# Two narrow first jobs, a last unit in halves, and an earlier 2 MB load in a fused attention kernel

## The chip, the cores and the metric

One core of one Trainium2 chip. The metric is device time in microseconds (us), the median over several executions of the whole program. Every run lists the mean granted clock of TensorE (1.0 is full speed). In the profiles PE is TensorE (matmuls), PEld its weight loads, ACT is ScalarE, DVE VectorE, POOL GpSimd, and SP SyncE, which issues most loads and stores. Ratios are the mean time of one kernel's fast runs over the mean of the other's in the same rounds on the same chip, so they are not quite the ratio of the medians quoted beside them.

## The reference

Two attention blocks over 2048 tokens, 1024 features and 32 heads of 32, results joined:

```python
# A: full softmax attention
scores = einsum('bhqd,bhkd->bhqk', q, k) * Dh ** (-0.5)
o = einsum('bhqk,bhkd->bhqd', softmax(scores), v)
out_A = o.transpose(0, 2, 1, 3).reshape(B, S, D) @ wo
# B: four segments of 512, causal attention in each, plus a memory M, z of the earlier ones
a_mem = (phi(q) @ M) / (phi(q) @ z + 1e-6)
o = g * a_mem + (1 - g) * a_dot          # g = sigmoid(beta)
# ... M and z are then updated from phi(k) and v; out_B = o @ wo
```

## The kernel before

A scheduler written in Python decides, while the program is built, the order of every instruction on every engine. It plans a chain of 621 score batches: PE multiplies QA by KA into PSUM (the buffer that matmuls write), ACT takes the exponential into a PT slot, PE multiplies PT by V and by ones (the row sums). Between the batches it places projection jobs (K, Q, V), output jobs and the memory work of block B. WoB holds the 2 MB of output weights of block B. Numbers in `par` steer the scheduler.

```python
par = dict(..., wob=80, oks=(1, 3, 5), pd=4, od=4, slk=0.3, ...)

def first_x(self):                        # the first four token tiles
    ...
    yield self.warm(8)                    # 8 matmuls of 512 columns on zeros, result unused
    for t in range(4):
        # 8 transposes of tile t into PSUM; after t == 1: self.warm(4)
        # DVE copies the tile to xA
    ...
def job(self, due, mm, keys, out, ...):   # a projection: 8 groups of 4 matmuls, n columns
    for i in range(last + 1):
        yield do("PE", lambda e: mm(e, i, bank, 0, n, st, sp), ...)
    yield do(eng, out, ...)               # DVE copies the result out of PSUM

def finish(...):                          # last unit: whole 256 queries at once
    # transpose(256), reciprocal, transpose(256), multiply -> OTA

yield ("ev", ("pos", self.par["wob"]))    # at this step of the chain
yield do("SP", lambda e: e.dma_start(self.WoB[:, :, :], ...), kb=2048)   # 2 MB in one load
```

## Time and profile before

| | before |
|---|---|
| time, median of 3 | 1099.28 us (1098.48 to 1099.56) |
| span of the profiled run, clock | 1097.8 us, 1.0 |
| start, to the first exponential | 10.40 us |
| ACT's idle time between exponentials | 4.67 us in seven gaps |
| tail, after the last exponential | 7.3 us |

The prediction below shows ACT's timeline and the tail. Here is PE's timeline where the 2 MB load of WoB is in flight. Columns: start, length, engine, line, operation, tiles, count, and in brackets the idle time before it with what ended it.

```profile
157.55 0.28 PE L1214 MATMUL ps<-PT,ones 128*32 128x256 bf16 x3
158.84 0.27 PE L1214 MATMUL ps<-PT,ones 128*32 128x256 bf16 x1 [1.01 <-issue]
```

PE stops after three of four matmuls that belong together. Nothing that the profile shows is awaited ("issue"). The second is a stretch of DVE and POOL at about 385 us:

```profile
383.05 1.22 DVE L884 SCALAR_TENSOR_TENSOR PH<-KQB,PH 128x1024 bf16<-128x1024 bf16 x1
...
386.26 0.42 DVE L1109 TENSOR_TENSOR PT<-PT,mask 128x512 bf16<-128x512 bf16 x1
...
387.03 0.72 POOL L891 TENSOR_SCALAR Zb<-maskbd,Mf 128x128 bf16<-128x128 f32 x1
```

### The profile page before, as it was taken

Reading aid. Unit: us, or ns where it says so; the run is one execution under the profiler, and the core shown is the slowest. Engines: PE = TensorE matmul, PEld = TensorE weight load, DVE = VectorE, ACT = ScalarE, POOL = GpSimd, SP = SyncE. Lnnn points to the kernel's source line nnn. Section 1 sums busy time; section 2 is a strip of 40 time slices with the busy share of each in tenths; the row PEclk is TensorE's granted clock in tenths of the full one; section 3 lists DMA queues with packets and bytes.
Section 4 is the critical chain, followed back from the end, with each engine's and each line's share of the span. In section 5 each row is a group of like instructions: output and inputs, shape, how many; then the busy total and the mean of one; then the engine's idle time right before and its main releaser. Section 6 shows DMA issues by size and latency. Waiting matters only on the chain.

```text
span 1097.8 us, 54247 instructions
## 1 busy us (share of the span) xinstructions
PE 1038.0 (95%) x25233; PEld 538.1 (49%) x25233; DVE 748.0 (68%) x1569; ACT 1077.1 (98%) x1188; POOL 127.4 (12%) x231
## 2 busy tenths in 40 slices
PE   8999999998999999999999998999999999899998
PEld 4545444444454445544454554544455444544454
DVE  2366666565778778887878789887748769543334
ACT  6999999999999999999999999999999999999997
POOL 2011110101102011110101121111102111100000
PEclk9999999999999999999999999999999999999999
DMA  9622361243302232243212242331122221201011
GB/s 189 102 61 56 75 139 30 52 92 64 72 27 53 59 61 48 50 85 70 56 42 55 42 84 46 73 63 35 48 65 56 51 46 22 84 32 36 31 41 67
DMA packets 213767, 67.49 MB, mean 61 GB/s; under 512 B 202786, under 2 KB 210978, under 8 KB 213538
## 3 DMA queue, kind: packets, MB, share of 16 engines
q1 hardware_dynamic: 212066, 63.07, 27.0%
q8 instruction: 199, 3.26, 1.3%
q10 hardware_dynamic: 1472, 0.92, 0.3%
q14 instruction: 30, 0.25, 0.1%
HBM read 36.70 MB, written 8.39 MB: 41 GB/s over the span
## 4 chain that ended last, share of the span: by engine, by line
ACT 83%; PE 12%; DVE 3%; DMA 1%; issue 0%; DVEq 0%
ACT PT L1099 82%; PE ps L719 4%; PE ps L1214 3%; PE ps L1068 2%; PE ps L1303 2%; DMA VA<-VT 1%; ACT OTA L1099 1%; PE ps L598 0%; DMA VB<-VT 0%; DVE VT L724 0%; ACT OTB L1099 0%; DVE PH L1137 0%; PE ps L646 0%; PE ps L899 0%; DVE OD L1256 0%
## 5 line engine op out<-in xcount | busy, mean ns | idle before, releaser
L1099 ACT ACTIVATE PT<-ps 128x1024 bf16<-128x1024 f32 x1164 | 1056.1, 1171 | 4.7 <-PE ps L1068 4.0
L1214 PE MATMUL ps<-PT,ones 128*32 128x256 bf16 (+2 forms) x4784 | 283.0, 268 | 1.0 <-issue 1.0
L1214 PE MATMUL ps<-PT,VA 128*32 128x256 bf16 x4016 | 241.4, 274 | 3.7 <-ACT PT L1099 1.4
L1068 PE MATMUL ps<-QA,KA 32*128 32x256 bf16 x4096 | 209.6, 273 | 31.0 <-ACT PT L1099 25.8
L719 PE MATMUL ps<-xB,WB 128*32 128x512 bf16 x3072 | 203.3, 381 | 3.4 <-DVE outsb L1308 0.9
L719 PE MATMUL ps<-xA,WA 128*32 128x512 bf16 (+1 forms) x3232 | 203.0, 371 | 3.1 <-DVE KA L724 0.6
L1068 PEld LDWEIGHTS ps<-QA,KA 32*128 32x128 bf16 x4096 | 62.8, 92 | 204.5 <-ACT PT L1099 189.7
L1214 PEld LDWEIGHTS ps<-PT,ones 128*32 128x32 bf16 x4784 | 128.0, 97 | 32.7 <-issue 16.0
L1214 PEld LDWEIGHTS ps<-PT,VA 128*32 128x32 bf16 x4016 | 107.3, 96 | 40.6 <-issue 22.0
L719 PEld LDWEIGHTS ps<-xA,WA 128*32 128x32 bf16 x3232 | 74.7, 96 | 76.0 <-issue 25.9
L719 PEld LDWEIGHTS ps<-xB,WB 128*32 128x32 bf16 x3072 | 71.0, 96 | 75.1 <-issue 30.0
L1256 DVE COPY OD<-ps 128x512 f32<-128x512 f32 x127 | 86.6, 682 | 24.3 <-PE ps L1214 23.5
L1308 DVE CAST outsb<-ps 128x512 bf16<-128x512 f32 x56 | 38.7, 690 | 77.9 <-PE ps L1303 75.5
L1111 POOL TENSOR_TENSOR PT<-PT,mask 128x256 bf16<-128x256 bf16 x64 | 46.6, 729 | 356.1 <-ACT PT L1099 354.0
L724 DVE CAST VT<-ps 128x512 bf16<-128x512 f32 x64 | 44.1, 688 | 63.1 <-PE ps L719 53.1
L724 DVE CAST KQB<-ps 128x512 bf16<-128x512 f32 x64 | 44.1, 689 | 54.2 <-PE ps L719 53.4
L1303 PE MATMUL ps<-WoB,OTB 128*32 128x512 bf16 x1024 | 67.2, 381 | 1.3 <-DVE OD L1256 1.0
L855 POOL COPY VZ<-VB 64x256 bf16<-64x256 bf16 x64 | 30.5, 476 | 299.7 <-DMA VB<-VT 256.8
L1262 DVE STREAM_TRANSPOSE OD<-Rall 128x256 f32<-128x256 f32 x127 | 55.7, 440 | 2.9
L1259 DVE STREAM_TRANSPOSE Dt<-OD 128x256 f32<-128x256 f32 x127 | 55.2, 436 | 2.2
L1303 PE MATMUL ps<-xA,OTA 128*32 128x512 bf16 x832 | 53.2, 381 | 0.0
L1214 PE MATMUL ps<-PT,VB 128*32 128x192 bf16 (+2 forms) x768 | 44.5, 240 | 4.8 <-DVE OD L1256 2.6
(111 smaller groups left out, 885.2 us busy)
## 6 DMA issues: line engine op xcount, KB each, us to landing
WB<-in_B_wk_dram SPq DMA_DIRECT2D x32, 256.0 KB, 3.0
WB<-in_B_wq_dram SPq DMA_DIRECT2D x32, 256.0 KB, 2.9
WB<-in_B_wv_dram SPq DMA_DIRECT2D x32, 256.0 KB, 3.1
out_dram<-outsb SPq DMA_DIRECT2D x63, 128.0 KB, 1.8
WA<-in_A_wqkv_dram SPq DMA_DIRECT2D x23, 256.0 KB, 3.3
WoB<-in_B_wo_dram SPq DMA_DIRECT2D x1, 2048.0 KB, 10.7
xA<-in_A_wo_dram SPq DMA_DIRECT2D x1, 2048.0 KB, 9.2
OTA<-in_A_x_dram SPq DMA_DIRECT2D x2, 256.0 KB, 5.0
```

What stands on the lines that cost most here:

```text
L719: ins = e.matmul(self.ps[32 * c:32 * c + 32, bank, lo:hi], W[:, i, 32 * c:32 * c + 32], x(i)[:, lo:hi], start=st, stop=sp)
L724: return e.tensor_copy(dst, self.ps[:, bank, 0:n])
L855: yield do("POOL", lambda e, j=j: e.tensor_copy(self.VZ[H * j:H * j + H, j:4:2, :], V[0:H, j:4:2, 0:P]), r=[("VB", n % 2)], w=["VZ"], cost ...
L1068: ins = e.matmul(out, l, r, start=a, stop=z)
L1099: yield do("ACT", lambda e: e.activation(to, self.ps[:, pr[0]:pr[1] + 1, 0:n], ACTF.Exp, scale=sc), r=[("ps", bk) for bk in pr], w=keys, c ...
L1111: yield do("POOL", lambda e: e.tensor_tensor(d, d, m, ALU.mult), r=keys + ["mask"], w=keys, cost=0.4 + sz * 0.0014, prio=0)
L1214: ins = e.matmul(out, l, r, start=st, stop=sp)
L1256: yield do("DVE", lambda e: e.tensor_copy(OD[:, :], self.ps[:, OB, :]), r=[("ps", OB)], w=[("OD", x), ("Rb", x)], cost=dve(2 * QU), prio=0 ...
L1259: yield do("DVE", lambda e: e.transpose(Dt[:, :], Rb), r=[("Rb", x)], w=[("Dt", x)], cost=dve(QU), prio=self.par["fp"], hold=0.15)
L1262: yield do("DVE", lambda e: e.transpose(Rb.rearrange("p (a b) -> p a b", b=32), self.spread(Rc)), r=[("Rc", ui % 64)], w=[("Rb", x)], cost ...
L1303: ins = e.matmul(self.ps[32 * c:32 * c + 32, bank, lo:hi], lhs(j)[:, 32 * c:32 * c + 32], W(j)[:, lo:hi], start=st, stop=sp)
L1308: return f(self.outsb[ob][:, :], self.ps[:, bank, :])
```

## The change

Its intent: begin the chain sooner, by letting the first K and Q jobs run on 128 tokens as soon as these are there; end it sooner, by normalising and projecting the last unit in two halves; and new numbers for the scheduler, which ask for WoB 20 steps sooner.

```diff
-    par = dict(... wob=80, oks=(1, 3, 5), pd=4, od=4, slk=0.3, ...)
+    par = dict(... wob=60, oks=(1, 4, 6), pd=6, od=0, slk=0.2, xp=0, wm=1, ...)
 def first_x(self):
-                yield self.warm(4)
+                yield self.warm(self.par["wm"])
 def job(...):
-        for i in range(last + 1):
+        for r, (lo, hi, xk, ev) in enumerate(ranges or [(0, n, [], None)]):
+            if ev:
+                yield ("ev", ev)
+            for i in range(last + 1):
+                fn = lambda e, ...: mm(e, i, bank, lo, hi, st, sp)
 # streams of group 0
-            streams = [[K and Q jobs], [V jobs]]
+            streams = {"K": todo[:1], "Q": todo[1:2], "rest": ..., "V": ...}
+            if g == c == 0 and w != "V":
+                ranges = [(0, P, [("xA", 0, t0)], None), (P, 2 * P, [("xA", 0, t0 + 1)], ("xt", 0, t0 + 1))]
 def finish(...):                          # last unit
-            # transpose(256), reciprocal, transpose(256), multiply
+            for tt in range(2):           # the same four on 128 queries, then
+                Q.fire(("finh", tt))      # the output jobs of this half may end
 # ... cut: bookkeeping of the events, order of the last output jobs
```

More of the change, by code (lines that the diff above doesn't have):

```diff
@@ L405 @@
 class Kernel:
-    par = dict(b=(16, 12, 9), mem=0, memM=2, span=60, rate=0.6, ahead=28, sl=7, pv=14, ob=4, lead=6, b0=1, bpos=16, wob=80, mg=0.05, off=0, oks=(1, 3, 5), sh=4, pd=4, o0=4, od=4, run=4, po=(1, 1), fp=2, fil=0.65, fs=0.15, ta=2, td=40, pvw=3, pvs=3, slk=0.3, pat=0.0, kh=3, mk=(0, 1, 1), mp=0, pe=3, tk=(0.5, 1))
+    par = dict(b=(16, 12, 9), mem=0, memM=2, span=60, rate=0.6, ahead=28, sl=7, pv=14, ob=4, lead=6, b0=1, bpos=16, wob=60, mg=0.05, off=0, oks=(1, 4, 6), sh=4, pd=6, o0=4, od=0, run=4, po=(1, 1), fp=2, fil=0.65, fs=0.15, ta=2, td=40, pvw=3, pvs=3, slk=0.2, pat=0.0, kh=3, xp=0, wm=1, mk=(0, 1, 1), mp=0, pe=3, tk=(0.5, 1))
     def __init__(self, nc, A_x, A_wqkv, A_wo, B_x, B_wq, B_wk, B_wv, B_wo, B_beta, out):
@@ L637, in first_x, with back @@
         pairs = yield acq(self.pairs, 3)
+        def back():
+            for t in range(4):
+                yield ("ev", ("xt", 0, t))
+                if t % 2:
+                    Q.give(self.pairs, [pairs[t // 2]])
+            Q.fire(("xA", 0))
+        Q.spawn(back())
         yield do("DVE", lambda e: e.memset(self.PT[:, 0, :], 0.0), w=[("PT", 0)], cost=0.3, prio=0)
@@ L647, in f @@
                 return ins
-            yield do("PE", f, r=[("XS", t), "ident"], w=[("ps", b)], cost=0.65, prio=0, mode=FULL)
+            yield do("PE", f, r=[("XS", t), "ident"], w=[("ps", b)], cost=0.6, prio=0 if t < 2 else self.par["xp"], mode=FULL)
             if t == 1:
-                yield self.warm(4)
+                yield self.warm(self.par["wm"])
                 Q.give(self.pairs, [pairs[2]])
@@ L654, in first_x @@
             Q.spawn(self.one(do("DVE", lambda e, s=src, d=dst: e.tensor_copy(d, s), r=[("ps", b)], w=[("xA", 0, t)], cost=0.6, prio=0), t))
-        for t in range(4):
-            yield ("ev", ("xt", 0, t))
-            if t % 2:
-                Q.give(self.pairs, [pairs[t // 2]])
-        Q.fire(("xA", 0))
     def one(self, op, t):
@@ L680, in rest_x, with job @@
             self.Q.fire(("xA", c))
-    def job(self, due, mm, keys, out, okey, wkeys, scale=None, eng="DVE", cost=None, okeys=(), gate=None, n=512):
+    def job(self, due, mm, keys, out, okey, wkeys, scale=None, eng="DVE", cost=None, okeys=(), gate=None, n=512, ranges=None):
         Q = self.Q
@@ L687, in job @@
         last = len(keys) - 1
-        for i in range(last + 1):
-            if gate and gate[0] == i:
-                yield ("ev", gate[1])
-            h = n // 2
-            st, sp = i == 0, i == last
-            fn = lambda e, i=i, st=st, sp=sp: mm(e, i, bank, 0, n, st, sp)
-            half = ((lambda e, i=i, st=st: mm(e, i, bank, 0, h, st, False)), (lambda e, i=i, sp=sp: mm(e, i, bank, h, n, False, sp)))
-            yield do("PE", fn, r=keys[i] + list(wkeys), w=[("ps", bank)], cost=N512 * n / 512, half=half if n == 512 else None,
-                     prio=(lambda: self.jprio(due)) if i == 0 else (lambda: min(self.jprio(due), self.par["run"])), mode=COL)
-            if i == 0 and last:
-                self.under.add(bank)
-            elif i == last:
-                self.under.discard(bank)
+        for r, (lo, hi, xk, ev) in enumerate(ranges or [(0, n, [], None)]):
+            if ev:
+                yield ("ev", ev)
+            for i in range(last + 1):
+                if gate and gate[0] == i:
+                    yield ("ev", gate[1])
+                w, m = hi - lo, (lo + hi) // 2
+                st, sp = i == 0 and not r, i == last and hi == n
+                fn = lambda e, i=i, st=st, sp=sp, lo=lo, hi=hi: mm(e, i, bank, lo, hi, st, sp)
+                half = ((lambda e, i=i, st=st: mm(e, i, bank, 0, m, st, False)), (lambda e, i=i, sp=sp: mm(e, i, bank, m, n, False, sp)))
+                yield do("PE", fn, r=(xk or keys[i]) + list(wkeys), w=[("ps", bank)], cost=N512 * w / 512 if w > P else 0.06,
+                         half=half if w == 512 else None,
+                         prio=(lambda: self.jprio(due)) if st else (lambda: min(self.jprio(due), self.par["run"])), mode=COL)
+                if st and last:
+                    self.under.add(bank)
+                elif sp:
+                    self.under.discard(bank)
         if eng == "any":
@@ L714, in pvprio, with proj @@
         return 5 if len(self.slots.items) < self.par['sl'] else self.par['pv']
-    def proj(self, due, W, wkey, x, xkeys, dst, dkeys, scale=None, n=512):
+    def proj(self, due, W, wkey, x, xkeys, dst, dkeys, scale=None, n=512, ranges=None):
         def mm(e, i, bank, lo, hi, st, sp):
@@ L725, in out @@
             return e.tensor_scalar(dst, self.ps[:, bank, 0:n], scale, None, ALU.mult)
-        return (yield from self.job(due, mm, [xkeys] * NI, out, dkeys, [wkey], n=n))
+        return (yield from self.job(due, mm, [xkeys] * NI, out, dkeys, [wkey], n=n, ranges=ranges))
     def turn(self, dst, src, r, w, prio=3):
@@ L754, in a_prep @@
         if g == 0:
-            streams = [[t for t in todo if t[0] != "V"], [t for t in todo if t[0] == "V"]]
+            streams = {"K": todo[:1], "Q": todo[1:2], "rest": [t for t in todo[2:] if t[0] != "V"], "V": [t for t in todo if t[0] == "V"]}
         else:
-            streams = [todo]
-        for i, st in enumerate(streams):
+            streams = {"all": todo}
+        for i, st in streams.items():
             Q.spawn(self.a_stream(g, st, due, ("stream", g, i)))
-        for i in range(len(streams)):
+        for i in streams:
             yield ("ev", ("stream", g, i))
@@ L771, in a_stream @@
         kind = {"K": 0, "Q": 1, "V": 2}
+        if done[2] == "rest":
+            yield ("ev", ("stream", g, "K"))
+            yield ("ev", ("stream", g, "Q"))
         for w, c, t0, t1 in todo:
@@ L774, in a_stream @@
             yield ("ev", ("WA", k, g))
-            for t in range(t0, t1):
+            ranges = None
+            if g == c == 0 and w != "V":
+                ranges = [(0, P, [("xA", 0, t0)], None), (P, 2 * P, [("xA", 0, t0 + 1)], ("xt", 0, t0 + 1))]
+            for t in range(t0, t0 + 1 if ranges else t1):
                 yield ("ev", ("xt", c, t % 4))
@@ L790, in a_stream @@
                 op = yield from self.proj(d, self.WA[k], ("WA", k), x, xk, dst[:, cs], [(w + "A", b, i) for i in h],
-                                          QSC if w == "Q" else None, P * (t1 - t0))
+                                          QSC if w == "Q" else None, P * (t1 - t0), ranges)
                 for i in h:
@@ L1244, in finish @@
             o = self.ps[:, OB, 0:QU]
-            yield do("DVE", lambda e: e.transpose(Dt[:, :], self.ps[:, OB, QU:2 * QU]), r=[("ps", OB)], w=[("Dt", x)], cost=dve(QU), prio=-5, hold=0.15)
-            yield do("DVE", lambda e: e.reciprocal(Rc, Dt[:, 0:QU:32]), r=[("Dt", x)], w=[("Rc", ui % 64)], cost=0.15, prio=-5, hold=0.15)
-            yield do("DVE", lambda e: e.transpose(Rb.rearrange("p (a b) -> p a b", b=32), self.spread(Rc)),
-                     r=[("Rc", ui % 64)], w=[("Rb", x)], cost=dve(QU), prio=-5, hold=0.15)
             g, qb = u[1], u[2]
-            yield do("DVE", lambda e: e.tensor_tensor(self.OTA[:, g, QU * qb:QU * qb + QU], o, Rb, ALU.mult),
-                     r=[("ps", OB), ("Rb", x)], w=[("OTA", g, qb // 2)], cost=dve(QU), prio=-5)
+            for tt in range(2):
+                c = slice(P * tt, P * tt + P)
+                R = Rc[:, 4 * tt:4 * tt + 4]
+                yield do("DVE", lambda e, tt=tt, c=c: e.transpose(Dt[:, c], self.ps[:, OB, QU + P * tt:QU + P * tt + P]), r=[("ps", OB)],
+                         w=[("Dt", x)], cost=dve(P), prio=-5, hold=0.15)
+                yield do("DVE", lambda e, c=c, R=R: e.reciprocal(R, Dt[:, c.start:c.stop:32]), r=[("Dt", x)], w=[("Rc", ui % 64)], cost=0.15,
+                         prio=-5, hold=0.15)
+                yield do("DVE", lambda e, c=c, R=R: e.transpose(Rb[:, c].rearrange("p (a b) -> p a b", b=32), self.spread(R)),
+                         r=[("Rc", ui % 64)], w=[("Rb", x)], cost=dve(P), prio=-5, hold=0.15)
+                yield do("DVE", lambda e, c=c, tt=tt: e.tensor_tensor(self.OTA[:, g, QU * qb + P * tt:QU * qb + P * tt + P], o[:, c], Rb[:, c], ALU.mult),
+                         r=[("ps", OB), ("Rb", x)], w=[("OTAh", tt)], cost=dve(P), prio=-5)
+                Q.fire(("finh", tt))
             Q.fire(("rc", ui))
@@ L1318, in out_A @@
         parts = [(tt, half) for tt in range(2) for half in range(2)]
+        if qb == NQ - 1:
+            parts = [(0, 1), (1, 1), (0, 0), (1, 0)]
         if qb >= NQ - 2:
@@ L1329, in out_A @@
             ns = slice(512 * half, 512 * half + 512)
-            Q.spawn(self.out_rows(due, lambda j, q0=q0: self.OTA[:, j, q0:q0 + P], [[("OTA", j, qb // 2)] for j in range(NG)],
+            Q.spawn(self.out_rows(due, lambda j, q0=q0: self.OTA[:, j, q0:q0 + P], [[("OTA", j, qb // 2)] for j in range(NG - 1)] + [[("OTAh", tt) if last else ("OTA", NG - 1, qb // 2)]],
                                   lambda j, ns=ns: self.WoA[:, j, ns], [("xA", 0, 0)], q0, 512 * half,
-                                  (NG - 1, ("fin", "A", NG - 1, qb)) if last else None, "ACT" if last and i % 2 else "SP"))
+                                  (NG - 1, ("finh", tt)) if last else None, "ACT" if last and i % 2 else "SP"))
             due += 2
@@ L1355, in out_ahead @@
                             [("part", i)] + over, [("xA", 0, 0)])
-        yield ("ev", ("fin", "A", NG - 1, qb))
+        last = qb == NQ - 1
+        yield ("ev", ("finh", tt) if last else ("fin", "A", NG - 1, qb))
         ob, = yield acq(self.outs, 1, d)
-        yield from self.job(-99, lambda e, j, *a: mm(e, NG - 1, *a), [[("OTA", NG - 1, qb // 2)]],
+        yield from self.job(-99, lambda e, j, *a: mm(e, NG - 1, *a), [[("OTAh", tt) if last else ("OTA", NG - 1, qb // 2)]],
                             lambda e, bank, eng: e.tensor_tensor(self.outsb[ob][:, :], self.ps[:, bank, :], part, ALU.add),
```

## The prediction

No term of its sum is among them; it stands as -0.5 - 1.1 - 0.55 + 0.35 = -1.8. Readings of the trace before: one exponential of 1024 columns took 1.02 us, the transposes started 0.107 and later 0.056 us apart, DVE operations on 256 columns took 0.42 to 0.45 us. The 0.30 us for three of the four halved operations in the tail was the author's estimate. The +0.35 does not hang on it: it comes of the issue time of 68 matmuls at 0.215 us for four (32 took 1.72 us, from 1091.10 on).

> **What bounds the kernel now.** I began with the page's busy times, then read ACT's timeline over the whole span, because the busiest engine is the only one whose idle time is worth anything.
>
> ```profile
> PE 1038.0 (95%) x25233; PEld 538.1 (49%) x25233; DVE 748.0 (68%) x1569; ACT 1077.1 (98%) x1188; POOL 127.4 (12%) x231
> ```
>
> ACT, which takes the exponentials, is busy 98% of 1097.8 us, and the chain that ended last lies on it for 83%. The change removes no exponential, so only ACT's idle time can shrink. ACT's timeline merges what runs back to back; the bracket gives the idle time before each stretch:
>
> ```profile
> 10.40 1.94 ACT L1099 ACTIVATE WoB<-ps 128x1024 bf16<-128x1024 f32 x2 [6.62 <-PE ps L1068]
> 13.00 5.69 ACT L1099 ACTIVATE WoB<-ps 128x1024 bf16<-128x1024 f32 x6 [0.65 <-PE ps L1068]
> ...
> 38.33 17.65 ACT L1099 ACTIVATE PT<-ps 128x1024 bf16<-128x1024 f32 x19 [1.11 <-PE ps L1068]
> ...
> 159.80 345.97 ACT L1099 ACTIVATE PT<-ps 128x512 bf16<-128x512 f32 x382 [1.08 <-PE ps L1068]
> 505.97 246.16 ACT L1099 ACTIVATE PT<-ps 128x1024 bf16<-128x1024 f32 x272 [0.20 <-PE ps L1068]
> 752.63 58.47 ACT L1099 ACTIVATE PT<-ps 128x1024 bf16<-128x1024 f32 x64 [0.50 <-PE ps L1068]
> 811.33 1.94 ACT L1099 ACTIVATE PT<-ps 128x1024 bf16<-128x1024 f32 x2 [0.24 <-PE ps L1068]
> 814.16 276.33 ACT L1099 ACTIVATE PT<-ps 128x1024 bf16<-128x1024 f32 x304 [0.89 <-PE ps L1068]
> 1093.89 1.07 ACT L1308 CAST outsb<-ps 128x512 bf16<-128x512 f32 x2 [3.40 <-PE ps L1303]
> ```
>
> So there are three places: the start before the first exponential (10.40 us), seven gaps inside (0.65 + 1.11 + 1.08 + 0.20 + 0.50 + 0.24 + 0.89 = 4.67 us), and the tail after the last one (814.16 + 276.33 = 1090.49 to the end at 1097.76, 7.27 us). What is left, 1097.76 - 10.40 - 4.67 - 7.27 = 1075.4 us, is work that stays. Everything the change can win lies in 22.3 us: it cannot reach 2% (22 us).
>
> [...]
> - [...] 1024 elements: [...] The trace has 1.02, and 0.91 to 0.95 apart. [...]
> - [...] The trace's transposes (128 columns) start 0.107 apart until 5.9 us and 0.056 apart after. [...]
> - [...] 256 elements: [...] the trace has 0.42 to 0.45. [...]
> - [...] the 1.08 gap at 159.80 follows 1.01 us of PE idle with "issue" as its reason, in the middle of a PV step; the 2 MB load of WoB (issued 149.99, landed 160.70) is in flight, and the instruction queue's packets, about 5.5 us apart on the whole, are 8.6 apart there (147.99, 156.55).
>
> **The change at the start.** The views are DVE's timeline and the PE instructions beside it.
>
> ```profile
> 5.73 1.30 DVE L654 COPY xA<-ps 128x1024 bf16<-128x1024 bf16 x2 [4.54 <-PE ps L646]
> 8.20 0.43 DVE L724 CAST KA<-ps 128x256 bf16<-128x256 f32 x1 [1.17 <-PE ps L719]
> 9.08 0.42 DVE L725 TENSOR_SCALAR QA<-ps 128x256 bf16<-128x256 f32 x1 [0.45 <-PE ps L719]
> 9.61 1.29 DVE L654 COPY xA<-ps 128x1024 bf16<-128x1024 bf16 x2
> 12.07 0.42 DVE L724 CAST KA<-ps 128x256 bf16<-128x256 f32 x1 [1.17 <-PE ps L719]
> ```
>
> Two copies bring token tiles 0 and 1 (5.73 to 6.42, 6.34 to 7.03); K starts at 7.09 after both, its 8 groups of 4 matmuls start 0.11 apart, Q's 8 follow, QA is cast at 9.08, and the first scores, behind 16 transposes, start at 9.96.
>
> In the changed order K runs on tile 0 from 6.42 + 0.06 = 6.48, its second range from 7.09 (8 x 0.057 = 0.46, so the last group starts at 7.49), Q's 16 groups from 7.55, last start 8.40, end 8.62 (0.22 as the transposes). QA: 8.67 to 9.09. Only 8 transposes now stand before the scores, so they start at about 9.15, and the first exponential 0.44 later as now: 9.6 instead of 10.40, **0.8 earlier**.
>
> Not all of it is kept. Tile 3's transposes move behind the scores (9.48 to 9.93), so its copy still ends near 10.87 (before 10.90). K's second range then needs 0.46 instead of 0.86: KA cast at 11.6, the second scores at 12.08 (before 12.55), exponentials at 12.5. The first two end at 9.6 + 1.94 = 11.5, so the 0.65 gap grows to 1.0. The next Q (16 x 0.057) leads to the third scores at 14.03 (before 14.46). From there ACT has a backlog: the start is worth **-0.45**. The next gap, 1.11 before 38.33, is PE waiting for the transposing DMA of the last V tile (issued 32.36, landed 37.41). Its cast moves with PE, so the gap should move too; with one group of 4 fewer between it and the scores, -0.05. Together **-0.5**.
>
> **The change in the middle.** The parameters (less slack, WoB asked for 20 steps sooner, output jobs due at once) do not change work, only the order. ACT needs about 1.85 us a score batch and the scores take PE 0.33, so other PE work above some 1.5 between two batches eats backlog. In the order before, the gaps 0.24 and 0.89 follow batches with 32 matmuls of 512 columns plus 2 and 6 groups of 256: 8 x 0.215 + 2 x 0.107 = 1.93 and 2.36 us. Counted this way over all 621 batches, the new order has none above 1.71, and those two stand in the first 26 batches as before, without a gap. **-1.1.** Of the other 1.78 us (1.08, 0.20, 0.50), the first is a fetch behind WoB, which now comes some 33 us earlier and may do it again; the other two are DVE running late. I take 1.2 of 1.78 to come back: **-0.55**.
>
> **The change in the tail.**
>
> ```profile
> 1091.10 1.90 PE L1303 MATMUL ps<-xA,OTA 128*32 128x512 bf16 x32
> 1091.33 0.45 DVE L1245 STREAM_TRANSPOSE Dt<-ps 128x256 f32<-128x256 f32 x1 [1.48 <-PE ps L1214]
> 1091.82 0.20 DVE L1246 RECIPROCAL Rall<-Dt 128x8 f32<-128x8 f32 x1
> 1092.05 0.45 DVE L1247 STREAM_TRANSPOSE OD<-Rall 128x256 f32<-128x256 f32 x1
> 1092.53 0.42 DVE L1250 TENSOR_TENSOR OTA<-ps,OD 128x256 bf16<-128x256 f32 x1
> ...
> 1093.01 0.61 PE L1350 MATMUL ps<-xA,OTA 128*32 128x512 bf16 x8
> ```
>
> The whole normalisation takes 1.68 us (1091.33 to 1093.01), but PE is filling 1091.10 to 1092.82 with the 32 matmuls of an unfinished output job: it loses only 0.19. Halved, four ops of 0.30, 0.18, 0.30, 0.30 plus the same steps between them give the first half after 1.25 us, at 1092.5, the second at 1093.7. But the new order puts one more output job (32 matmuls, 1.72 us) behind the last scores: after the last PV come 32 + 4 + 16 + 4 + 12 = 68 matmuls, 17 x 0.215 = 3.66 us from about 1091.0, so the last group starts at 1094.45 (before: 1093.66) and PE, not the halves, sets the end. ACT's last copy then runs 1094.9 to 1095.5 and its store is issued at 1095.5 (before 1095.00 and 1095.03, landing 1097.22); one eviction and one store are still behind it. **+0.35**, part of the later issue being slack against the other queue.
>
> **Sum:** -0.5 - 1.1 - 0.55 + 0.35 = -1.8: 1099.3 to **1097.5 us**.
>
> **Rivals.**
> 1. The start is swallowed: the V tile's DMA lands when traffic lets it (5.05 us here, 2.5 to 3.2 for the three before it). For: it stands behind a 256 KB load. Against: that load is issued by the same PE progress. Then 1098.0.
> 2. The halves do shorten the tail by 0.5: if the extra job fitted in PE's gaps before the last exponential. Against: the order. Then 1096.6.
> 3. The new order meets new waits: 2 MB landing among group loads, DVE late elsewhere. The old one had 2.9 us of gaps after 100 us, so a new one can have 3 to 4: 1099 to 1099.5.
> 4. With 1 warming matmul instead of 4 the PE clock falls back and the first jobs take twice as long: +1. Against: PE has no gap above 0.2 us there.
>
> **Range and chances.** The start is sure to 0.3, the tail to 0.4, the middle to 1.2; repeats of the kernel before spread over 1.1 us. Eight in ten: 1096.0 to 1099.2. Faster by over 2%: 0.005; slower: 0.005; within 2%: 0.99.
>
> **What would show it.** First exponential near 9.6, gap before the third near 1.0, no gap for want of PE at 810 to 815, a fetch gap near 115 to 130 or none, and after the last exponential 7.5 to 7.7 us with PE busy to 1094.9 on this clock. I am wrong if the middle gaps sum to over 4 us, or if the tail falls below 7.

## The result, and the profile after

| | before | changed |
|---|---|---|
| median | 1099.42 us (6 runs) | 1103.84 us (6 runs, 1101.35 to 1106.82) |
| ratio, 95% interval | | 1.004 (1.0022 to 1.0057) |
| granted clock of the runs | | 0.992 to 0.998, never 1.0 |
| profiled run: span, clock | 1097.8 us, 1.0 | 1105.1 us, 0.992 |
| start, to the 29th exponential | 38.33 us | 38.93 us |
| from there to the end of the last exponential | 1052.2 us | 1058.8 us |
| tail | 7.3 us | 7.3 us |

The change is slower by 0.4%, outside my range. The profiled run is the slowest of its six. The profile's busy line of the changed kernel, against the one in the prediction:

```profile
PE 1045.0 (95%) x25518; PEld 542.3 (49%) x25518; DVE 750.4 (68%) x1573; ACT 1078.1 (98%) x1188; POOL 126.0 (11%) x231
```

ACT's work is the same within 1 us. PE has 285 more matmuls. So the question is again where ACT idles. Its timeline in the changed kernel:

```profile
9.32 1.94 ACT L1112 ACTIVATE WoB<-ps 128x1024 bf16<-128x1024 f32 x2 [5.53 <-PE ps L1081]
13.15 5.96 ACT L1112 ACTIVATE WoB<-ps 128x1024 bf16<-128x1024 f32 x6 [1.90 <-PE ps L1081]
...
38.93 17.67 ACT L1112 ACTIVATE PT<-ps 128x1024 bf16<-128x1024 f32 x19 [0.91 <-PE ps L1081]
...
129.80 3.40 ACT L1112 ACTIVATE PT<-ps 128x1024 bf16<-128x1024 f32 x4 [3.15 <-PE ps L1081]
133.96 1.94 ACT L1112 ACTIVATE PT<-ps 128x1024 bf16<-128x1024 f32 x2 [0.76 <-PE ps L1081]
136.37 3.89 ACT L1112 ACTIVATE PT<-ps 128x1024 bf16<-128x1024 f32 x4 [0.47 <-PE ps L1081]
141.34 25.46 ACT L1112 ACTIVATE PT<-ps 128x1024 bf16<-128x1024 f32 x28 [1.07 <-PE ps L1081]
...
396.30 1.94 ACT L1112 ACTIVATE PT<-ps 128x1024 bf16<-128x1024 f32 x2 [0.94 <-PE ps L1081]
398.83 1.94 ACT L1112 ACTIVATE PT<-ps 128x1024 bf16<-128x1024 f32 x2 [0.59 <-PE ps L1081]
401.37 112.52 ACT L1112 ACTIVATE PT<-ps 128x1024 bf16<-128x1024 f32 x124 [0.60 <-PE ps L1081]
```

The first exponential is early, as predicted, but the next gap is 1.90 and the gain is gone by 13.15. Two clusters of gaps in the middle are new: 3.15 + 0.76 + 0.47 + 1.07 = 5.45 us from 129.80 on, and 0.94 + 0.59 + 0.60 = 2.13 us from 396.30 on. The windows view around the first cluster shows what PE did (length, busy time of PE, PEld, DVE, ACT and POOL with counts, granted clock, busy share of the DMA engines, GB/s):

```profile
core 0: us, PE busy (x) PEld busy (x) DVE busy (x) ACT busy (x) POOL busy (x), PEclk, DMA share, GB/s
120.42:123.84 3.42, 3.42 (x96) 2.06 (x88) 0.68 (x2) 3.42 (x5) 0.00 (x0) 1.00 0.99 313
123.84:127.25 3.41, 1.50 (x37) 0.61 (x31) 0.69 (x1) 2.81 (x4) 1.19 (x2) 1.00 1.11 359
127.25:130.67 3.42, 2.17 (x36) 1.36 (x35) 1.34 (x3) 0.87 (x1) 0.14 (x1) 0.50 1.24 89
130.67:134.08 3.41, 3.20 (x70) 1.90 (x70) 1.85 (x5) 2.65 (x5) 0.50 (x1) 0.50 0.30 4
...
137.49:140.91 3.42, 3.42 (x48) 0.93 (x40) 2.23 (x6) 2.76 (x3) 0.00 (x0) 0.50 0.00 0
140.91:144.32 3.41, 3.41 (x80) 1.69 (x80) 0.96 (x2) 2.97 (x4) 0.00 (x0) 1.00 0.33 76
```

While the DMA engines are full (busy share 1.11), PE is busy for only 1.50 of 3.41 us. With the next window the clock is 0.50, and stays there for four windows, 13.65 us, until one is busy throughout. The trace's record of the granted clock has half a clock for 13.65 us from 127.26 and for 3.41 us from 396.91, and the full clock for 122.88, 256.00 and 706.56 us before, between and after: 4, 1, 36, 75 and 207 times 3.413. So in this trace the clock changes only in steps of 3.41 us, and the windows here are laid on these. The window before a half clock need not be empty: 44% busy was enough the first time, and 35% (from 393.50) the second. The PE timeline in the first of these two:

```profile
125.06 0.28 PE L1227 MATMUL ps<-PT,VA 128*32 128x256 bf16 x2
127.74 0.40 PE L1227 MATMUL ps<-PT,VA 128*32 128x256 bf16 x2 [2.40 <-issue]
```

It is the same picture as at 158.84 before, with 2.40 us instead of 1.01. And the start of the changed kernel has it twice in small:

```profile
10.60 0.40 PE L726 MATMUL ps<-xA,WA 128*32 128x128 bf16 x13 [0.23 <-DVE xA L662]
11.72 0.46 PE L726 MATMUL ps<-xA,WA 128*32 128x128 bf16 x19 [0.72 <-issue]
...
16.50 0.29 PE L726 MATMUL ps<-xA,WA 128*32 128x256 bf16 x4 [0.58 <-issue]
```

I counted the trace's records of PE (matmuls, weight loads and the few of its sequencer, in order of start) before each of these stops: 449, 705 and 5825 in the changed kernel, 7105 before. All four are 193 past a multiple of 256. (Smaller or later stops lie at 193 to 195 past, as one of 0.21 us at 257.22 in the changed kernel: a count from the records can be off by a few.) The instruction queue moved 201 packets and 3.29 MB, 16 KB each, for 51,262 such records: one packet for 255 of them. So **theory A**: PE runs out of fetched instructions, because its next packet is stuck behind data loads; when the stop leaves a clock window too empty, the clock halves and the cost multiplies. **Theory B**: the new order itself, or the narrow ranges, leave PE without work, and the load is a bystander. The late DVE at 396 is a cause of its own in either case (**C**).

### The profile page after: what moved, and what is told of

Same layout as the page of the kernel before. It is cut to its first block, busy times and chain, and to the rows that moved or that the text cites. A ratio compares the mean times of both kernels' runs of the same rounds, so it can differ in the third digit from the quotient of the medians.

```text
span 1105.1 us, 54825 instructions
## 1 busy us (share of the span) xinstructions
PE 1045.0 (95%) x25518; PEld 542.3 (49%) x25518; DVE 750.4 (68%) x1573; ACT 1078.1 (98%) x1188; POOL 126.0 (11%) x231
## 3 DMA queue, kind: packets, MB, share of 16 engines
q8 instruction: 201, 3.29, 1.3%
## 4 chain that ended last, share of the span: by engine, by line
ACT 67%; PE 26%; DVE 4%; DMA 1%; issue 1%; ACTq 0%; DVEq 0%
ACT PT L1112 66%; PE ps L726 12%; PE ps L1227 6%; PE ps L1081 5%; PE ps L1322 2%; DMA WA<-in_A_wqkv_dram 1%; DVE OD L1275 1%; ACT OTA L1112 1%; DMA VA<-VT 0%; DVE VT L731 0%; DVE PT L1122 0%; DMA VB<-VT 0%; DVE PH L1150 0%; DVE we L1149 0%; ACT OTB L1112 0%
## 5 line engine op out<-in xcount | busy, mean ns | idle before, releaser
L726 PE MATMUL ps<-xA,WA 128*32 128x512 bf16 (+2 forms) x3424 | 204.9, 359 | 3.9 <-issue 1.3
L726 PE MATMUL ps<-xB,WB 128*32 128x512 bf16 (+1 forms) x3120 | 205.8, 380 | 2.8 <-DVE KA L731 0.8
L726 PEld LDWEIGHTS ps<-xA,WA 128*32 128x32 bf16 x3424 | 77.0, 96 | 78.5 <-issue 28.5
L1322 PE MATMUL ps<-WoB,OTB 128*32 128x512 bf16 (+1 forms) x1044 | 67.6, 377 | 0.5 <-DVE KQB L731 0.4
```

The costliest lines, as they stand in the source:

```text
L726: ins = e.matmul(self.ps[32 * c:32 * c + 32, bank, lo:hi], W[:, i, 32 * c:32 * c + 32], x(i)[:, lo:hi], start=st, stop=sp)
L1322: ins = e.matmul(self.ps[32 * c:32 * c + 32, bank, lo:hi], lhs(j)[:, 32 * c:32 * c + 32], W(j)[:, lo:hi], start=st, stop=sp)
```

## The experiments

All kernels gave correct results. "29th" is the start of the 29th exponential, behind the start and the wait for the last V tile of the group.

**1. The changed kernel, WoB back at step 80.** `wob=60` to `wob=80`, nothing else.

> The changed kernel with one number put back: the 2 MB load of WoB is asked for at step 80 again, not 60. Theory A (the bursts of loads around 117 to 130 us starve PE's instruction fetch, the idle halves its clock for 13.65 us): no PE idle of over 2 us and no half clock near 127 us, at most a gap of about 1 us near 160 as before; about 1100 us. Theory B (the new order itself, not the load): the gaps of 3.15 + 0.76 + 0.47 + 1.07 us stay somewhere near; about 1103.5 us.

Measured: 1102.04 us (4 runs), ratio to before 1.0016 (0.9998 to 1.0033); profiled span 1099.4 against 1105.1. ACT's timeline:

```profile
56.15 157.14 ACT L1112 ACTIVATE PT<-ps 128x1024 bf16<-128x1024 f32 x173
...
390.29 1.94 ACT L1112 ACTIVATE PT<-ps 128x1024 bf16<-128x1024 f32 x2 [0.75 <-PE ps L1081]
```

The whole cluster at 129.80 is gone: one stretch of exponentials from 56 to 213 us. The stop moved with the load (now in flight from 150.54 to 161.38): PE stops for 0.92 us up to 163.89, 194 past a multiple of 256, and ACT has enough work waiting not to idle. That is theory A's outcome for this place. The cluster behind DVE (0.75 + 0.59 + 0.24) and its half window stay. The time came out 2 us above what A expected; both start and cluster C remain. The two spans do not compare the kernels: 1105.1 is the slowest of six runs and 1099.4 the fastest of four. What this experiment shows is in the trace, not in the time.

**2. The kernel before, WoB at step 60.** `wob=80` to `wob=60` in the old kernel.

> The kernel before with one number changed: WoB asked for at step 60. Theory A: a PE idle of 1 us or more near 125 us in the middle of a batch of work, with issue as its reason, at an instruction count that is 193 past a multiple of 256; if it is over 2 us, a half clock behind it; 1100.5 to 1104 us. Theory B: no such gap, 1099.4 us.

Measured: 1101.98 us (4 runs, 1100.76 to 1106.18), ratio 1.0018 (0.999 to 1.0047). The stop is there, after 5569 instructions (193 past a multiple of 256), at 125.14 us, but only 0.72 us long and without half a clock. This run's loss is mostly elsewhere: up to 248.15 us PE waited 1.44 us for a transposing DMA of PKt, and from 246.6 us on the clock was half for two windows. So the early load makes the stop, but its length is not fixed.

**3. The changed kernel, WoB in eight loads.** One `dma_start` of 2 MB becomes eight of 256 KB, four steps apart.

> The changed kernel with the 2 MB load of WoB cut into 8 loads of 256 KB, 4 steps apart, the first at step 60. Theory A: no fetch gap near 125 us, no half clock there, 1099 to 1100.5 us (the start's fetch gaps and the late DVE near 395 may stay). Theory B: 1103.5 us.

Measured: 1103.13 us (4 runs), ratio 1.0024 (1.0001 to 1.0047). No stop near 125 us and no half clock there: A's mechanism again. But the time did not follow. The 29th came at 39.33 (the start's two stops were 0.94 and 1.15 us here), and the moved order had a new wait for DVE with a half window at 444.7 us. A miss in the sum, not in the mechanism.

**4. The changed kernel without the narrow ranges.** `if g == c == 0 and w != "V":` becomes `if False:`.

> The changed kernel, but the first K and Q jobs not cut in ranges of 128 tokens. If the narrow ranges (twice the instructions for the same work) make PE run out of fetched instructions in the start, its idle of 0.72 and 0.58 us at 11.7 and 16.5 us goes; the first exponential comes about 0.4 us later than in the changed kernel, the gap before 38.9 us about equal. The burst near 117 to 130 us stays, so 1102 to 1104 us, unless the boundary of the instruction blocks now falls beside it: then about 1099.5.

Measured: 1100.47 us (4 runs), ratio 1.0006 (0.9979 to 1.0033). Both stops of the start are gone. The first exponential comes at 9.33, no later than with the ranges; the third at 12.65 instead of 13.15, the 29th at 37.70 instead of 38.93. I had expected the first to lose 0.4: it did not, because PE needs 2.36 us for the 128 narrow matmuls where it needs 1.93 for the 64 wide ones, and starts them 0.44 sooner (5.97 against 6.41). In these two traces the ranges bring the first exponential nothing and cost 1.2 us at the 29th.

**5. The start of the change alone**, in the old order.

> The kernel before with the start of the change alone (two streams, ranges of 128 tokens, one warming matmul); the order after the first 40 rows of PE is that of before. If the narrow ranges starve PE of instructions: idle of 0.6 to 1.0 us at about 11.7 and 16.5 us, both 193 past a multiple of 256 instructions; first exponential 9.3, the 29th (behind the V tile's wait) at 38.6 to 39.3 against 37.9 to 38.3 of the old start; rest as before, so 1099.5 to 1101 us. If my prediction was right about the start: 29th at 37.4 to 37.9, 1098.8 us.

Measured: 1101.37 us (4 runs), ratio 1.0018 (0.9996 to 1.0041). Stops after 449 and 705 instructions again, 0.34 and 0.32 us. First exponential 9.58, third 13.04, 29th 38.55. The starts of several runs, with the time from which the clock was full, since that differs from run to run and shifts everything (the order alone is experiment 7 below):

| kernel | clock full from | 1st | 3rd | 29th |
|---|---|---|---|---|
| before | 5.90 | 10.40 | 13.00 | 38.33 |
| start of the change alone | 5.67 | 9.58 | 13.04 | 38.55 |
| new order alone (old start) | 3.99 | 9.71 | 12.31 | 36.80 |
| changed, no ranges (4) | 4.12 | 9.33 | 12.65 | 37.70 |
| changed | 4.38 | 9.32 | 13.15 | 38.93 |

The first two rows share the old order: the first exponential is 0.82 us earlier, the third not at all. The last three share the new order: there the start as a whole costs 2.1 us at the 29th, and 1.2 of these are the ranges. Of the first exponential's gain little is left where the clock comes early: the old start had it at 9.71 to 9.76 in the four traces with the clock full from 3.99 to 4.24, the changed start at 9.32 to 9.37 in the four from 4.38 to 4.45. PE then also reaches its boundaries sooner and stops longer (0.58 to 1.15 us). The run of this experiment also lost 1.31 us of ACT at the fetch stop behind WoB (PE: 1.22) and 1.68 us near 361, behind a window of half clock; the second I did not follow.

**6. The tail of the change alone**, in the old order (8 rows, that is steps of PE's planned order, differ).

> The kernel before with the tail of the change alone (halves of 128 queries), old order: 8 rows of PE differ. Without the extra output job behind the last scores the halves should take effect: from the last exponential's end to the end of the span 6.8 us against 7.3 of before; 1098.9 us. If PE's queue sets the end in any case: 7.3 and no difference.

Measured: 1099.64 us (5 runs), ratio 0.9995 (0.9979 to 1.0012). From the end of the last exponential to the end of the span 7.25 us, against 7.31. The first half is ready 1.2 us after the chain's start (1091.49 to 1092.70), but PE is still in its 32 filling matmuls and takes it up at 1093.00, 1.51 us after that start; before it took up the whole after 1.68 (1091.33 to 1093.01). The second half follows after 2.37 us (1093.86). The rival expectation held: no effect.

**7. The new order alone**: the old kernel with the five changed numbers.

> The kernel before with the five changed numbers of the order alone (WoB at 60, oks, pd, od, slk). If the order with the early load is what costs: a fetch gap near 125 us at 193 past a multiple of 256 and a gap behind DVE near 390 us with half a clock after one or both, the gaps near 811 to 814 us smaller: 1101 to 1104 us. If the start were the cause: 1098 us.

Measured: 1097.67 us (4 runs: 1097.17, 1097.24, 1098.10, and 1102.10 at clock 0.995), ratio 0.9991 (0.9967 to 1.0015). This surprised me: the order with the early load is the fastest kernel seen, in most of its runs. The stop is there, after 5569 instructions, but 0.22 us long.

**8. Streams and halves without ranges, old order** (17 rows of PE differ).

> Start of the change without the narrow ranges (two streams, tile 3's transposes behind the scores, one warming matmul), tail in halves, old order and WoB at 80: 17 rows of PE differ from before. First exponential 9.3, 29th at 37.7 (as in the run without ranges), middle as before, tail 6.8: 0.2 to 0.6 from the start and 0.5 from the tail, so 1098.3 us against 1099.4, unless the order of the tail or a fetch gap behind WoB moves.

Measured: 1099.86 us (6 runs), ratio 1.0 (0.9984 to 1.0017). Same as before; my 1098.3 was too low. In the trace the tail took 7.26 us instead of 6.8, and the 29th came at 38.26 instead of 37.7 (the clock was full only from 6.61).

**9. The changed kernel once more, unaltered.**

> The changed kernel, unaltered, a second time. Is the fetch gap at 127.7 us with its 13.65 us of half clock there every time, or does its size vary with how late the instruction packet comes? If fixed: a gap of 2.4 us of PE idle after 5825 instructions again, five half windows, 1103.8 us. If it varies: the same boundary (5825), but an idle anywhere from 0.2 to 2.5 us, and times from 1101 to 1107 us that go with the granted clock (0.998 for one half window, 0.992 for five).

Measured: 1100.84 us (6 runs, 1099.71 to 1106.29), ratio 1.0026 (1.0007 to 1.0046). The profiled run has the stop after the same 5825 instructions, with another length:

```profile
125.78 0.29 PE L1227 MATMUL ps<-PT,VA 128*32 128x256 bf16 x2 [0.39 <-issue]
```

So the same instruction stream stops for 2.40 us in one execution and for 0.39 in another. The records of the instruction queue tell why. In the changed kernel half of the packets start within 0.6 us of PE's crossing of a boundary, three quarters within 1.1 (5057 was crossed at 108.23, and a packet started at 108.51). Behind the WoB load they come later:

| kernel | boundary crossed | packet starts | late by | PE goes on | after the packet's start | PE idle |
|---|---|---|---|---|---|---|
| before | 152.42 | 156.55 | 4.1 | 158.84 | 2.3 | 1.01 |
| changed | 120.06 | 125.17 | 5.1 | 127.74 | 2.6 | 2.40 |
| changed, again | 120.11 | 123.32 | 3.2 | 125.78 | 2.5 | 0.39 |
| changed, no ranges | 118.80 | 123.02 | 4.2 | 125.39 | 2.4 | 1.30 |
| before, WoB early | 119.47 | 122.84 | 3.4 | 125.14 | 2.3 | 0.72 |
| order alone | 117.79 | 121.05 | 3.3 | 123.30 | 2.3 | 0.22 |
| order alone, again (12) | 117.84 | 121.87 | 4.0 | 124.39 | 2.5 | 1.26 |

PE goes on 2.3 to 2.6 us after its packet starts, and one block lasts it 5 to 6 us here. A packet up to about 3 us late costs nothing (3.1 in experiment 11, without a stop); beyond that about each microsecond is a microsecond of idle PE. How late it is varies by 2 us in one and the same kernel. Two cases bound this. In the start, where a block of narrow matmuls lasts under 4 us, a packet 1.5 us late already cost 0.32 (experiment 11). And in experiment 1 the packet was only 1.1 late, but took 3.07 us instead of about 1, so PE stopped all the same.

The second trace of the changed kernel holds another lesson. Its clock is half from 130.72 to 134.14, after a window in which PE was busy for 1.97 of 3.41 us, because it waited 1.05 us for ACT and 0.80 for DVE. ACT ran through that half window without a gap. So other waits than the fetch can halve the clock too, and half a clock need not cost time. The two sets of this one kernel lie 3 us apart (1103.84 and 1100.84), so the times of experiments 1, 3 and 4 (1100.5 to 1103.1) do not show any of them to be faster than the changed kernel.

**10. The new order alone, WoB in eight loads.**

> The old start and tail with the order of the change, WoB's 2 MB cut into 8 loads of 256 KB, 4 steps apart. If a long burst is what delays the packets: no idle over 0.5 us at 193 past a multiple of 256 near 115 to 165 us, clock 1.0 in nearly all runs, 1097 to 1097.8 us, and no run over 1100. If the split moves the order badly (it does change 1032 rows): new gaps behind DVE elsewhere, 1099 us.

Measured: 1098.65 us (5 runs, 1098.40 to 1100.67), ratio 0.9992 (0.9979 to 1.0005). No stop over 0.15 us at any of its 198 boundaries. But no run held the full clock (0.998 in four, 0.997 in the profiled one, whose half windows begin at 246.35 and 444.32 us; up to 442.57 PE had waited 0.97 us for DVE). Steadier, not shown to be faster.

**11. The changed kernel, the loads of the other token tiles held back** until tile 3 is copied. Slower on purpose.

> The changed kernel with the transposing loads of the other 12 token tiles held back until tile 3 has been copied (10.5 us instead of 4.55). Slower on purpose. If these loads delay the instruction packet in the start: the first packet comes near 7.5 to 8.3 us (boundary at 7.3 us) instead of 9.41, and PE does not stop after 449 instructions; second pair of exponentials at 12.3 us instead of 13.15. If the packet's time has nothing to do with them: packet at 9.4, idle 0.7 us after 449 as before.

Measured: 1104.72 us (one run). The first packet starts at 8.50 instead of 9.41; its boundary was crossed at 7.54 (7.28 in the changed kernel), so it is 1.0 late instead of 2.1. PE's timeline over the place of the stop, and ACT's:

```profile
10.86 1.52 PE L727 MATMUL ps<-xA,WA 128*32 128x128 bf16 x96 [0.22 <-DVE xA L662]
```

```profile
12.77 1.02 ACT L1113 ACTIVATE WoB<-ps 128x1024 bf16<-128x1024 f32 x1 [1.25 <-PE ps L1082]
```

No stop after 449 instructions: 96 matmuls in one piece, KA cast at 11.54, where my prediction had said 11.6. The expected 7.5 to 8.3 for the packet was slightly missed, with the first loads landing until 8.29. The third exponential came at 12.77, a little under half of the way from 13.15 to 12.3. The clock was full from 5.79 here, so experiment 5 (5.67) is the nearer comparison: packet at 9.24, boundary at 7.54, stop of 0.34, third exponential at 13.04. The edit also moved the order: the second scores now stand behind the next Q. The second stop, after 705 instructions, stayed at 0.32 us; its packet came at 12.49, 1.5 late, with the held-back loads (issued from 10.84) now in flight. So it takes both: the data loads delay the packet, and the ranges bring PE to the boundary before it is there; without the ranges (experiment 4) the same loads made no stop.

**12. The new order alone, again.**

> The old start and tail with the order of the change, a second time, to see whether 1097.7 us and its one slow run of four (1102.1 at clock 0.995) repeat. The idle after 5569 instructions (0.22 us in the first trace) should be 0 to 1.3 us; most runs 1097.2 to 1098.2 at clock 1.0, one in four or five 2 to 5 us longer at a lower clock. If the first result was luck: median over 1099 us.

Measured: 1099.28 us (6 runs, 1097.73 to 1100.61), ratio 0.9995 (0.9982 to 1.0007). Here the profiled run had 1.26 us of idle after 5569 instructions, half a clock for two windows, and gaps of 1.15 + 0.60 + 0.46 us. Two of six runs held clock 1.0, at 1097.7 and 1097.8. So the four runs of experiment 7 were partly luck.

**13, 14, 15. The new order alone, with the burst elsewhere**: WoB at step 80; at step 100; in eight pieces, eight steps apart, from step 44.

> Old start and tail, new order, WoB at 80 as in the kernel before. If the order's term of my sum (-1.65 us) was right and only the packets spoil it: 1097.5 us at clock 1.0, fetch idle under 1 us near 150 to 165. If the gap behind DVE near 390 us comes back with its half clock (0.75 + 0.59 + 0.24 us as in the changed kernel with WoB at 80): 1098.8 us, clock 0.998 in most runs.

> As the run before, WoB at step 100. Loads beside it are other ones, so the packet's delay differs: 3 to 5 us late means an idle of 0 to 2.4 us at one boundary near 190 to 205 us, under 3 us late means none. 1097.5 us without one, 1098.5 to 1101 with one.

> New order, WoB in 8 pieces of 256 KB, 8 steps apart from step 44 on. No idle over 0.3 us at 193 past a multiple of 256 anywhere after 20 us (as in the split 4 steps apart). 1097.5 us if the order is good as it stands; 1098.6 us if the gap behind DVE near 390 or 447 us halves the clock as it did there.

Measured: 1099.97 (6 runs, ratio 1.0005), 1100.44 (6 runs, 1.0006) and 1101.90 us (6 runs, 1.0015). The first had stops of 1.23 and 0.56 us behind its WoB load. The other two had none there, but stops of 0.97 us at 251.9 and 1.27 us at 719.6, each behind a transposing load of xB that took about 9 us (242.4 to 251.5; 710.9 to 719.7). The packets were 3.7 and 4.0 us late. So it is not WoB alone: another load of that length can do it, and the kernel before has such a stop too, 0.74 us at 716.96. All three have the gap behind DVE at about 390 us, each with half a clock. The stop of experiment 14 cost ACT nothing, so there it is this gap that eats the order's gain. Experiment 14 shows the place (columns as before):

```profile
384.77 0.89 DVE L1109 TENSOR_TENSOR PT<-PT,mask 128x512 bf16<-128x512 bf16 x1
385.58 1.43 DVE L884 SCALAR_TENSOR_TENSOR PH<-KQB,PH 128x1024 bf16<-128x1024 bf16 x1
386.03 1.57 POOL L891 TENSOR_SCALAR Zb<-maskbd,Mf 128x128 bf16<-128x128 f32 x1
387.13 0.68 DVE L1256 COPY OD<-ps 128x512 f32<-128x512 f32 x1
387.96 0.35 PE L1214 MATMUL ps<-PT,VB 128*32 128x192 bf16 x4 [2.00 <-DVE OD L1256]
```

Against the lines of before: the mask takes 0.89 instead of 0.42, L884 1.43 instead of 1.22, POOL's Zb 1.57 instead of 0.72. In the new order these lie on top of each other; the OD copy comes late and PE waits 2.00 us. The changed kernel has the same durations at 392 to 395 us (0.89, 1.43 and 1.57) and a wait of 2.34. That POOL's operation beside them makes the DVE ones long is what the trace shows in part: L884 lost 0.21 us beside Zb, but the 256-column mask at 386.93, also beside Zb, took its usual 0.28. Over the whole trace of before, 512-column masks took 0.51 us in the median where they overlap POOL (13 of them) and 0.41 where they do not (19). What the three long DVE operations lost, 0.35 (1.04 instead of 0.69, just before these lines) + 0.47 + 0.21 = 1.03 us, is half of the 2.00; I estimate the other half to be the order, which puts all three before the OD copy.

**16 and 17. Taking the overlap away**: as 14, with all masks on DVE (`mk=(1, 1, 1)`); with Mb and Zb on DVE.

> As the run with the new order and WoB at step 100, but all mask multiplies on DVE, none on POOL. There, near 385 us, DVE operations that lay beside POOL's took 0.89 instead of 0.42 us (mask, 512 columns), 1.04 instead of 0.69 and 1.43 instead of 1.22, and PE then waited 2.0 us for a DVE copy. If that overlap makes the gap: these durations go back to 0.42, 0.69 and 1.22, no half clock near 390 us, 1098 us at clock 1.0 (64 more DVE operations of 0.3 us, which may make other gaps since 2705 rows of PE move). If the gap comes of the order: it stays, 1100 us.

> As the run with the new order and WoB at step 100, but the two POOL operations that build Mb and Zb (0.48 and 1.57 us there) are on DVE. The 1024-column operation beside them (1.43 us) should go back to 1.22 to 1.25 us, the gap near 390 us shrink below 0.6 us without a half clock, 1098 to 1098.5 us. If the masks on POOL are enough for the gap: it stays above 0.6 us, 1099.5 to 1100.5 us.

Measured: 1111.78 (4 runs, ratio 1.0109) and 1109.63 us (6 runs, 1.0087). Far slower, and not for the reason in question: the moved order has places where PE does 8 to 10 us of other work between two score batches (ACT gaps of 2.91 and 7.31 us in the first, 1.99 and 6.06 in the second). At 385 to 390 us, though, the gap is gone in both. In 16, with no POOL operation beside it:

```profile
384.95 0.42 DVE L1109 TENSOR_TENSOR PT<-PT,mask 128x512 bf16<-128x512 bf16 x1
```

No ACT gap over 0.15 us from 341 to 438 us in the first, none over 0.21 from 356 to 507 in the second, and no half clock. In 17 the mask still takes 0.89 beside POOL's masks, but L884, now free of POOL, takes 1.22. So the long durations come with the overlap and go with it. That the overlap alone makes the gap is not shown, since the order moved as well, and by the sum above it is about half of it.

No version beat the kernel before beyond doubt. The nearest are 7 and 12, the new order alone: 10 runs with a median of 1098.5, four of them at 1097.2 to 1097.8, three above 1100.

## Why the prediction was wrong, point by point

**The bound** was read rightly: ACT's work was unchanged within 1 us, and everything happened in start, gaps and tail. (Two neighbouring exponentials start 0.90 us apart in the median of the trace, a little less than the 0.91 to 0.95 that I read.)

**The start, -0.5.** The step to the first exponential was right for the clock of the trace it was read from (0.8 predicted, 0.82 in experiment 5 against before, 9.58 where 9.6 was predicted); where the clock comes on at about 4.4 us, only some 0.4 is left. The next step failed: "K's second range then needs 0.46 instead of 0.86". It needs that only if PE has the instructions. With twice as many for the same work PE crosses its first boundaries sooner than the packets can follow the token loads, and stops for 0.3 to 1.15 us twice. Measured for the start: +0.2 at the 29th exponential in the old order (38.55 against 38.33), +2.1 in the new one (38.93 against 36.80). Experiment 11 shows that with those loads held back KA comes as I had worked out.

**The middle, -1.1 and -0.55.** The gaps at 811 to 814 went, as counted, but two smaller ones of the same kind (0.18 and 0.37) came 9 us nearer to the end. The step that failed most is this sentence: "the first is a fetch behind WoB, which now comes some 33 us earlier and may do it again", taken at most at its old size of 1.08. I had its cause and its place right. I had not asked what sets its size: the packet was 5.1 us late instead of 4.1, PE idled 2.40 instead of 1.01, that left a clock window 44% busy, and half a clock for 13.65 us made 5.45 us of ACT idle out of it. Nor did I have the late DVE of the new order, in part its overlap with POOL, worth 0.6 us without a half clock and up to 2.1 with one. Instead of -1.65 the middle gave +6.7 in the profiled run (1058.8 against 1052.2), which was the slowest of its six, and +0.2 in the profile of experiment 9 (1052.4), where the stop was 0.39. The order alone gave -0.9 in one profile (1051.3) and +2.5 in the other (1054.6). So the start failed in every trace of the changed kernel, by about 1 us; the middle failed by 2 and 8 us in its two profiles of the unaltered kernel, and most of the difference is one packet (5.45 us of ACT idle behind it against 0.29).

**The tail, +0.35.** Measured 0.0 in the changed kernel, about nothing for the halves alone. PE's queue set the end as said; the store was issued 5.0 us after the last exponential, as worked out, but what follows it cost less.

**The rivals.** Rival 3 (new waits) was the right one, with 1.5 to 2 us above the sum instead of the 6.3 and 3.3 seen in the two sets. Rival 4 (the clock falls back) had the right mechanism in the wrong place (half a clock for 13.65 us from 127.26, after a window 44% busy). I looked for it only in the start. Of my two signs of being wrong one came: the gaps after the 29th exponential sum to 8.8 us in the profiled run (3.1 in that of experiment 9), while the tail did not fall below 7.

**The range.** "The middle to 1.2" took the spread of gaps from one profile at clock 1.0. A term that can set off the half clock has a long tail on one side. The two sets of the changed kernel differ by 3 us (1103.84 and 1100.84); both lie above my upper end of 1099.2. Of the kernel before's 41 runs beside the experiments 22 had a clock of 0.999 or 1.0 (1098.0 to 1099.9) and 19 a lower one (up to 1103.1); of the changed kernel's 12 none reached 0.999.

**What stays open.** Why a packet is 3.2 us late in one execution and 5.1 in another, and what halves the clock in the slower runs of the kernel before, whose profiled run had none of it. The split of a median into these causes is not shown either: each kernel has one profile per set, and in the other runs only the clock is known.

## What to carry to other kernels

When PE idles with "issue" as the reason, count its instructions there: here the stops shared a remainder modulo 256 (193 to 195) and a packet of the instruction queue came late before each (4.1 us before the stop of 1.01, 5.1 before that of 2.40), and that is how they were found to be fetches. What removed the stops here was fewer instructions for the same work (experiment 4) or shorter loads ahead of them (3 and 10); neither was shown to save time. With PE 95% and ACT 98% busy, a wait was not worth its own length here: ask whether it leaves a 3.4 us window of PE less than about half busy, because after such windows (0.31 to 0.44 busy, and some of 0.58 to 0.59) the clock was half here, and that cost a multiple (5.45 us of ACT for 2.40 of PE) or, where ACT had work waiting (experiment 9), nothing. Look at the clock of every run before trusting a median, and take a second profile of the same kernel before explaining the first. Narrower pieces that start sooner double the instructions; check that the pieces are not paid back in issue time (2.36 us for the 128 narrow matmuls against 1.93 for the 64 wide ones, and two stops of 0.3 to 1.15).

## What the traces show of fetching and of the clock

- PE ran on at all but two to four of some 200 boundaries in the traces before and after; but it stopped after 449 instructions, and after 5825, 5569, 7105 and others, 193 to 195 past a multiple of 256, and a packet 4 to 5 us late cost 1.0 to 2.4 us. One packet came for 255 records of PE, every 5.5 us on the whole (199 in 1097.8 us before).
- Packets that came during loads of 9 to 12 us were up to 5.1 us late, and PE stopped for up to 2.40 us.
- By the PE busy time in the traces, windows busy for a share of 0.31 (experiment 9, from 386.72), 0.35 and 0.44 (changed kernel) were followed by half a clock, windows at 0.55 (changed, from 11.20) and 0.57 (before, from 166.33) by the full one, and windows at 0.58 and 0.59 (experiment 10, from 440.91, and 2, from 243.19) by half a clock again, so busy time alone does not decide it. At half clock, windows with 2.17, 3.20 and 2.61 us busy of 3.41 did not bring the full clock back in the changed kernel; one of 3.42 did, and one of 3.29 of 3.40 (from 396.92).
- From an instruction packet's start to PE going on took 2.3 to 2.6 us in the seven stops of the table. A packet about 3 us late cost nothing where a block lasts PE 5 to 6 us (3.1 in experiment 11); in the start 1.5 us late cost 0.32.
